# A gated recurrence and a PReLU network on one core: first-chunk scores in halves and quads, keys transposed by VectorE and DMA, weights in wider pieces

## The chip, the cores and the metric

The kernel runs on one core of a Trainium2 chip. A core has TensorE for matrix products, VectorE and ScalarE for elementwise work, GpSimd, and SyncE, which only issues transfers; 16 DMA engines move data for all of them. The time is the device time of one execution in microseconds, as a median of several runs.

## The reference

Two parts follow each other. The first is a recurrence with a gate for every key dimension, over 4 batches x 8 heads, 768 positions, 48 dimensions; the second is a network with a PReLU.

```python
f = 1.0 / (1.0 + np.exp(-f_logit))
for t in range(S):
    state = f[:, :, t, :, None] * state + einsum('bhd,bhde->...', k[:, :, t], v[:, :, t])   # outer product
    y[:, :, t] = einsum('bhd,bhde->bhe', q[:, :, t], state)
x = y.transpose(0, 2, 1, 3).reshape(3072, 384)
h = x @ w_in                                   # 384 -> 2048
g = np.maximum(h, 0.0) + alpha * np.minimum(h, 0.0)
out = g @ w_out                                # 2048 -> 384
```

## The kernel before

Positions are cut into six chunks of 128 (NC = 6) and batches into two pairs, which gives 12 steps (bp, c), all first chunks (c = 0) ahead. A step goes through four stages written as generators: `prepare` (gates and their products), `carry` (what passes between blocks, and the state), `attend` (scores inside blocks, output y) and `network`. A string of letters sets the order in which the pieces of the stages are issued: P and Q are prepare of this and the next step, O is carry, S is attend, n is the network of the step before, a and w load the input weights, b and v the output weights. TensorE, VectorE and ScalarE follow this order exactly.

Within a chunk, scores are formed in blocks of 32 positions. The gate products between two positions of a block are built by quads of four positions: `qd` for pairs in one quad, and `us` for pairs in different quads, where one product is kept for every distance m between quads, up to seven.

```python
# prepare
q4 = us[:, :, 0:DB]...                       # distance 1
def earlier(m):                              # distance m from distance m-1, m = 2..7
    nc.vector.tensor_tensor(us[... UO[m] ...], us[... skip ...], fq[:, :, 1:1 + n]..., ALU.mult)
k4 = work.tile([128, W], F32, ...)           # k times the gates to the end of its quad
nc.vector.tensor_tensor(k4, k, kr..., ALU.mult)
# q3: q times the gates since the start of the block, ks, kh: k times the gates to the end of the block
```

In `carry`, the gated keys `ks` are transposed on TensorE and copied by ScalarE, and multiplied with the values:

```python
pk = pair(f"pk_{i}")
for u in range(U):
    for hp in range(HP):
        nc.tensor.transpose(pk[:, u, hp * 128:(hp + 1) * 128], ks[...], ident)
ksn = work.tile([128, U, HP * 128], F32, tag="ksn", ..., bufs=1)
for u in range(U):
    nc.scalar.copy(ksn[:, u], pk[:, u])
...
nc.tensor.matmul(pd[64 * par:64 * par + 64, cc, o:o + D],
                 lhsT=ksn[s_, u, hp * 128 + 64 * par:hp * 128 + 64 * par + 64], rhs=vs[...])
```

In `attend`, raw is k times qd, qu is k4 times us, and copies under a mask put the wanted parts into `ad`; `ad` and the other parts go into A, and A times the values gives py, then y. Ten small DMAs place y as xT for the network:

```python
nc.tensor.matmul(raw[...], lhsT=k[...], rhs=qd[r_, g])                       # 80 columns
nc.tensor.matmul(qu[...], lhsT=k4[...], rhs=us[r_, g, 4:UW])                 # 112 columns
for m in range(1, NB):                                                       # seven copies
    nc.vector.copy_predicated(ad[:, u, :, :, 4 * m:DB], mquad[...], qu[...])
...
(nc.sync if hd % 2 else nc.scalar).dma_start(out=xT[...], in_=y[p0:p0 + n, :, hd // 2])
```

The network multiplies xT with w_in (ph, eight groups of 12 matmuls), forms g on ScalarE and VectorE, and multiplies with w_out (po, 64 matmuls).

Both weights arrive as 64-bit words from which the kernel takes the float32 value in two parts: ScalarE and VectorE work out the leading and the remaining part of a piece of WP = 512 columns, and a GpSimd DMA with addition joins them:

```python
def both(n):
    nc.gpsimd.dma_start(out=flat[:, n:n + WP], in_=got.pop(n)[1], accum_op=ALU.add)
```

Of the kernel before, what the change touches and what calls it, by code (L numbers as in the profile page):

```python
# [8 lines left out]
F32 = mybir.dt.float32  # L9
I16 = mybir.dt.int16  # L10
# [11 lines left out]
U = 2  # L22
# [3 lines left out]
WP = 512  # L26
RAWS, TOPS, POWERS, LEADS = 5, 3, 2, 4
# [3 lines left out]
def kernel(  # L31
# [27 lines left out]

    nc = tc.nc  # L60
# [11 lines left out]
    NJ = C // DB  # L72
    UO = [0, 0]
    for m in range(1, NB):
        UO.append(UO[-1] + (DB if m == 1 else DB - 4 * m))
    UW = UO.pop()
    QO = [0]
# [46 lines left out]
    for m in range(1, NB):  # L124
        lo = UO[m] + (4 if m == 1 else 0)
        n = NB - m
        nc.gpsimd.tensor_copy(mquad[:, lo:lo + 4 * n].rearrange("p (i r) -> p i r", r=4),
                              inq[:, 0:n].unsqueeze(2).broadcast_to((128, n, 4)))
    ad = const.tile([128, U, 2, HP, DB], F32, tag="ad", name="ad")
# [12 lines left out]

    def load_weights(dst, src, name):

        flat = dst.rearrange("p a n -> p (a n)")
        ks = NK if dst is w_in_sb else 1
        per = flat.shape[1] // ks
        todo = [k * per + j for j in range(0, per, WP) for k in range(ks)]
        got = {}

        def upper(n):
            raw = work.tile([128, WP, 4], I16, tag="raw", name=f"{name}_raw{n}", bufs=RAWS)
            nc.sync.dma_start(out=raw.rearrange("p n four -> p (n four)")[:, 0:4 * WP - 1],
                              in_=src[:, n:n + WP].bitcast(I16)[:, 1:4 * WP])

            top = raw[:, :, 2]
            pos = work.tile([128, WP], I16, tag="pos", name=f"{name}_pos{n}", bufs=TOPS)
            nc.scalar.activation(pos, top, AF.Relu, bias=bias[:, 0:1], scale=8.0)
            neg = work.tile([128, WP], I16, tag="wneg", name=f"{name}_neg{n}", bufs=TOPS)
            nc.scalar.activation(neg, top.bitcast(U16), AF.Relu, bias=bias[:, 1:2], scale=8.0)  # L170
            got[n] = raw, pos, neg

        def lead(n):
            raw, pos, neg = got[n]
            t = work.tile([128, WP], BF16, tag="lead", name=f"{name}_lead{n}", bufs=LEADS)
            nc.vector.tensor_tensor(t, pos.bitcast(BF16), neg.bitcast(BF16), ALU.subtract)
            got[n] = raw, t

        def power(n):
            raw, t = got[n]  # L180
            p = work.tile([128, WP], BF16, tag="power", name=f"{name}_power{n}", bufs=POWERS)
            nc.vector.tensor_scalar(p.bitcast(I16), t.bitcast(I16), -128, None, ALU.bitwise_and)
            got[n] = raw, t, p

        def rest(n):
            raw, t, p = got[n]
            low = raw.bitcast(U32)[:, :, 0]
            nc.vector.scalar_tensor_tensor(flat[:, n:n + WP], low, 2.0 ** -36, p, ALU.mult, ALU.mult)

        def both(n):  # L190
            nc.gpsimd.dma_start(out=flat[:, n:n + WP], in_=got.pop(n)[1], accum_op=ALU.add)  # L191

        def uppers():
            for n in todo:
                upper(n)
                yield

        def rests():
            for i, n in enumerate(todo + [None]):
                if n is not None:  # L200
                    lead(n)
                if i:
                    rest(todo[i - 1])
                if n is not None:
                    power(n)
                if i:
                    both(todo[i - 1])
                yield

        return uppers(), rests()  # L210
# [10 lines left out]

    def fill():

        while True:
            b = bank("warm")
            nc.tensor.matmul(b[:, 0:256], lhsT=ones[:, 0:128], rhs=ones[:, 0:256], start=True, stop=True)
            yield

    def prepare(bp, c, x):
# [42 lines left out]
        us = x["us"] = work.tile([128, G, UW], F32, tag="us", name=f"us_{i}", bufs=1)  # L272
        q4 = us[:, :, 0:DB].rearrange("p g (i r) -> p g i r", r=4)
        for r in range(4):
            nc.scalar.copy(q4[:, :, :, r], qdv[r][:, :, :, 0])  # L275
        nc.vector.tensor_tensor_scan(ps, fs, ones, 0.0, ALU.mult, ALU.add)
# [16 lines left out]

        k4 = x["k4"] = work.tile([128, W], F32, tag="k4", name=f"k4_{i}", bufs=1)
        nc.vector.tensor_tensor(k4, k, kr.rearrange("p n r -> p (n r)"), ALU.mult)
        earlier(2)
# [7 lines left out]

        def started(j):
            js = slice(j, G, 2)
            nc.vector.tensor_tensor(q3[:, :, 2 * j].rearrange("p g (i r) -> p g i r", r=4), q4[:, js],  # L307
                                    pre[:, js, 0:NB].unsqueeze(3).broadcast_to((128, GC, NB, 4)), ALU.mult)
# [9 lines left out]
        earlier(3)  # L318
        ended(1)
        earlier(4)  # L320
        started(1)
        earlier(5)
        yield
        earlier(6)
        nc.vector.tensor_tensor(ks[:, :, 0], kh, f32[:, 1:G:2].broadcast_to((128, GC, DB)), ALU.mult)
        earlier(7)
        nc.vector.tensor_tensor(q3[:, :, 1], q3[:, :, 2], f32[:, 0:G:2].broadcast_to((128, GC, DB)), ALU.mult)
# [10 lines left out]
        for cc in range(NC2):  # L338
            for par in range(2):
                nc.scalar.copy(A[halves(cc)[1], :, par * HP:(par + 1) * HP, CH * cc:CH * (cc + 1)],  # L340
                               q3[rows(par)].rearrange("p (u h c) s t -> p u h c (s t)", h=HP, c=NC2)[:, :, :, cc, 0:CH])
        yield

    def carry(bp, c, x):
# [4 lines left out]
        for u in range(U):  # L349
            for hp in range(HP):  # L350
                for cc in range(NC2):
                    g = (u * HP + hp) * NC2 + cc
                    o = (u * HP + hp) * DB
                    for par in range(2):
                        r_ = rows(par)
                        nc.tensor.matmul(off[CH * cc:CH * cc + DB, par, o:o + DB],  # L356
                                         lhsT=kh[r_, g], rhs=q3[r_, g, 2], start=True, stop=True)
        for cc in range(NC2):
# [6 lines left out]
        pk = pair(f"pk_{i}")  # L365
        for u in range(U):
            for hp in range(HP):
                a = (u * HP + hp) * NC2
                nc.tensor.transpose(pk[:, u, hp * 128:(hp + 1) * 128], ks[:, a:a + 2].rearrange("p c s t -> p (c s t)"), ident)  # L369
        ksn = work.tile([128, U, HP * 128], F32, tag="ksn", name=f"ksn_{i}", bufs=1)  # L370
        for u in range(U):
            nc.scalar.copy(ksn[:, u], pk[:, u])
        yield
        pd = pair(f"pd_{i}")
        for u in range(U):
            for hp in range(HP):
                for cc in range(NC2):
                    for par in range(2):
                        o = (u * HP + hp) * D
                        s_ = halves(cc)[0]  # L380
                        nc.tensor.matmul(pd[64 * par:64 * par + 64, cc, o:o + D],  # L381
                                         lhsT=ksn[s_, u, hp * 128 + 64 * par:hp * 128 + 64 * par + 64],
                                         rhs=vs[bp][s_, cc, u, (2 * hp + par) * D:(2 * hp + par + 1) * D], start=True, stop=True)

        def moved(cc):
# [6 lines left out]
            for par in range(2):  # L392
# [3 lines left out]
                else:  # L396
                    nc.vector.tensor_copy(then[:, :, par:H:2], now)  # L397
# [5 lines left out]
    def attend(bp, c, x):  # L403
# [4 lines left out]

        for u in range(U):
# [16 lines left out]
            for hp in range(HP):  # L426
                for j in range(NJ):
                    g = (u * HP + hp) * NJ + j
                    for par in range(2):
                        r_ = rows(par)  # L430
                        nc.tensor.matmul(qu[DB * j:DB * (j + 1), par, hp * UW + 4:(hp + 1) * UW],  # L431
                                         lhsT=k4[r_, g * DB:(g + 1) * DB], rhs=us[r_, g, 4:UW], start=True, stop=True)
            for m in range(1, NB):
                lo = UO[m] + (4 if m == 1 else 0)
                n = DB - 4 * m
                nc.vector.copy_predicated(  # L436
                    ad[:, u, :, :, 4 * m:DB],
                    mquad[:, lo:lo + n].bitcast(I32).unsqueeze(1).unsqueeze(1).broadcast_to((128, 2, HP, n)),
                    qu[:, :, 0:HP * UW].rearrange("p r (h x) -> p r h x", h=HP)[:, :, :, lo:lo + n])
# [26 lines left out]
        xT = x["T"] = work.tile([128, NK, T], F32, tag="xT", name=f"xT_{i}")  # L466
        for hd in range(H):
# [10 lines left out]
    def network(bp, c, x):  # L478
# [21 lines left out]
        for f in range(NF):  # L500
            for u in range(U):
                nc.tensor.matmul(po[u][:, 0:DM], lhsT=gs[f // 2][:, f % 2, u * C:(u + 1) * C], rhs=w_out_sb[:, f],  # L502
                                 start=(f == 0), stop=(f == NF - 1))
            if f % 4 == 3 and f != NF - 1:
                yield
        for u in range(U):
# [3 lines left out]
            nc.sync.dma_start(out=out[t0:t0 + C], in_=o)  # L510
        yield
# [7 lines left out]
        "P2 a2 P2 w a2 w P O w P a w S2 O w Q S2 a w a S a S Q w2",  # L519
        "a P w a w a P w n P a n w b v w S b v n b n O v b v n b v S P S n b O b v n b S v2 n2 S n b v Q b v b n v b v2 Q3 S n Q",  # L520
        "n2 O n S n2 S Q S n S O n2 Q n Q2 n P S n S Q n Q",
        "n S n2 S Q n2 O n S n S Q n O Q2 n Q S2 Q n3",
    )
    usual = "O n2 S n2 S2 n O n Q n Q n S n2 S Q n S Q2 n Q"
# [10 lines left out]
    with tc.manual_schedule(engines={mybir.EngineType.PE, mybir.EngineType.DVE, mybir.EngineType.Activation}):  # L535
        prep, car, att, net = begin(0)
        filling = fill()
        before = None
        for n in range(len(steps) + 1):
            coming, carried, following, after = begin(n + 1)  # L540
            on = pieces | {"P": prep, "O": car, "S": att, "z": filling, "n": before, "Q": coming}
# [60 lines left out]
```

## Time and profile before

| What | Value |
|---|---|
| Time, median of 3 runs | 659.77 us (658.13 to 659.81) |
| Span of the profiled execution | 658.4 us |
| PE (matmul) busy | 615.5 us, 93% |
| PEld (weight load) busy | 458.0 us, 70% |
| DVE (VectorE) busy | 420.2 us, 64% |
| ACT (ScalarE) busy | 267.0 us, 41% |
| POOL (GpSimd) busy | 69.9 us, 11% |
| Moved by DMA | 53.03 MB, 81 GB/s on average |

The profile calls TensorE PE and its weight loads PEld, VectorE DVE, ScalarE ACT, GpSimd POOL and SyncE SP; a q behind the name is the engine's queue of DMA issues. A line such as `L486 ph<-xT,w_in_sb` is the instruction of line 486 that writes ph from xT and w_in_sb. "Idle before" is the time in which the engine waited for it, and the arrow names what ended the wait. The granted clock is the share of TensorE's full clock that it was allowed in a stretch.

The shares are averages over a start, in which weights are prepared and little can be multiplied, and a long steady part. They have to be read by stage.

### The profile page before, as it was taken

To read this page: it belongs to the slowest core of one execution; us is meant where nothing else is said; L and a number is where in the kernel's file an instruction comes from. 1 tells how busy PE (TensorE), PEld (TensorE's weight loads), DVE (VectorE), ACT (ScalarE), POOL (GpSimd) and SP (SyncE) were. 2 spreads that over 40 slices of the span, in tenths; PEclk is the share of its full clock that TensorE was granted. 3 is DMA by queue.
4 is the path that set the end of the run, shared out by engine and by line. 5 is a ranking of instruction groups with operands and counts; after the bars stand their busy time and mean duration, and the time that the engine had idled before them with its cause. 6 is when DMAs were issued, how large, how long until landed. Compare 5 with 4: busy or idle time off the path is not lost.

```text
span 658.4 us, 17032 instructions
## 1 busy us (share of the span) xinstructions
PE 615.5 (93%) x7392; PEld 458.0 (70%) x7392; DVE 420.2 (64%) x897; ACT 267.0 (41%) x493; POOL 69.9 (11%) x109
## 2 busy tenths in 40 slices
PE   0548899999999999999999999999999999999997
PEld 0436766866876876876876876876876786786874
DVE  5999889693863685685585586486387486360220
ACT  5855882543443242451451550550460451431210
POOL 8222332000010000000000001001001000000000
PEclk9857999999999999999999999999999999999999
DMA  6979986122212122112013113023023011001000
GB/s 225 302 207 269 282 233 159 35 65 73 66 37 68 35 52 87 33 40 86 28 53 81 31 62 81 26 66 80 26 66 81 26 34 25 26 2 25 24 1 24
DMA packets 29129, 53.03 MB, mean 81 GB/s; under 512 B 4320, under 2 KB 16864, under 8 KB 29056
## 3 DMA queue, kind: packets, MB, share of 16 engines
q0 software_dynamic: 9616, 27.92, 15.4%
q1 hardware_dynamic: 13584, 21.63, 10.6%
q10 hardware_dynamic: 5856, 2.40, 1.7%
q8 instruction: 58, 0.95, 0.6%
q14 instruction: 15, 0.12, 0.1%
HBM read 36.21 MB, written 4.72 MB: 62 GB/s over the span
## 4 chain that ended last, share of the span: by engine, by line
PE 84%; issue 7%; POOL 4%; DVE 2%; ACT 1%; DMA 1%; POOLq 0%
PE po L502 36%; PE ph L486 35%; PE py L456 3%; PE qu L431 3%; PE raw L416 3%; PE pk L369 2%; PE pd L381 2%; POOL w_in_sb L191 1%; PE off L356 1%; POOL w_out_sb L191 1%; DMA w_out_sb<-w_out_lead 1%; DVE us L289 0%; POOL vs L138 0%; ACT A L340 0%; POOL vs L247 0%
## 5 line engine op out<-in xcount | busy, mean ns | idle before, releaser
L486 PE MATMUL ph<-xT,w_in_sb 128*128 128x256 f32 x1152 | 264.3, 387 | 10.3 <-DMA xT<-y 10.3
L502 PE MATMUL po<-w_out_sb,g 128*128 128x384 f32 x768 | 253.0, 488 | 0.3 <-DMA w_out_sb<-w_out_lead 0.3
L486 PEld LDWEIGHTS ph<-xT,w_in_sb 128*128 128x128 f32 x1152 | 218.1, 192 | 44.7 <-DMA w_in_sb<-w_in_lead 11.3
L502 PEld LDWEIGHTS po<-w_out_sb,g 128*128 128x128 f32 x768 | 144.9, 190 | 97.7 <-DMA w_out_sb<-w_out_lead 0.9
L494 DVE SCALAR_TENSOR_TENSOR g<-neg,om,ph 128x256 f32<-128x256 f32 x192 | 83.1, 476 | 152.0 <-ACT neg L491 151.9
L491 ACT ACTIVATE neg<-ph 128x512 f32<-128x512 f32 x96 | 57.7, 601 | 152.8 <-PE ph L486 124.8
L508 ACT COPY o<-po 128x384 f32<-128x384 f32 x24 | 11.5, 478 | 115.2 <-PE po L502 115.2
L436 DVE COPY_PREDICATED ad<-mquad,qu 128x224 f32<-128x224 int32 (+6 forms) x168 | 50.3, 300 | 8.5 <-DVE ad L422 0.5
L465 ACT COPY y<-py 128x512 f32<-128x512 f32 x24 | 12.9, 591 | 81.2 <-PE py L456 81.2
L289 DVE TENSOR_TENSOR us<-us,fs 128x768 f32<-128x768 f32 (+2 forms) x72 | 44.5, 618 | 0.3
L422 DVE COPY_PREDICATED ad<-mraw,raw 128x256 f32<-128x256 int32 (+1 forms) x96 | 42.3, 441 | 2.7
L445 ACT COPY A<-ad 32x256 f32<-32x256 f32 x96 | 38.4, 400 | 3.8 <-DVE ad L436 2.5
L391 DVE TENSOR_TENSOR vs<-vs,f 48x768 f32<-48x768 f32 x20 | 19.1, 953 | 30.4 <-PE py L456 30.0
L275 ACT COPY us<-qd 128x256 f32<-128x256 f32 x48 | 29.6, 666 | 12.2 <-DVE qd L258 7.4
L258 DVE TENSOR_TENSOR qd<-qd,f 128x768 f32<-128x768 f32 (+2 forms) x36 | 27.1, 752 | 8.2 <-ACT qd L253 8.2
L340 ACT COPY A<-q 48x512 f32<-48x512 f32 x48 | 29.6, 617 | 6.3 <-DMA xT<-y 5.5
L237 POOL DMA_DIRECT2D k<-in_kT x11 | 8.4, 761 | 222.6 <-PE raw L416 197.6
L456 PEld LDWEIGHTS py<-A,vs 128*64 128x64 f32 x768 | 25.1, 145 | 7.2 <-issue 6.2
L431 PE MATMUL qu<-us,k 48*32 48x112 f32 x1536 | 26.4, 265 | 2.6 <-DVE us L289 1.7
L456 PE MATMUL py<-A,vs 128*64 128x64 f32 x768 | 26.9, 231 | 0.9 <-DVE vs L397 0.8
L356 PE MATMUL off<-q,kh 48*32 48x32 f32 x768 | 9.4, 199 | 18.3 <-DVE q L307 18.3
L416 PEld LDWEIGHTS raw<-qd,k 48*32 48x32 f32 x1536 | 18.1, 108 | 10.6 <-issue 10.2
(64 smaller groups left out, 451.1 us busy)
## 6 DMA issues: line engine op xcount, KB each, us to landing
w_in_raw<-in_w_in SPq DMA_DIRECT2D x12, 511.8 KB, 5.9
w_out_raw<-in_w_out SPq DMA_DIRECT2D x12, 511.8 KB, 5.8
f<-in_fT POOLq DMA_DIRECT2D x11, 512.0 KB, 4.1
q<-in_qT POOLq DMA_DIRECT2D x11, 512.0 KB, 4.1
k<-in_kT POOLq DMA_DIRECT2D x11, 512.0 KB, 4.3
out<-o SPq DMA_DIRECT2D x24, 192.0 KB, 1.9
vs<-in_v POOLq DMA_DIRECT2D x22, 192.0 KB, 3.5
w_in_sb<-w_in_lead POOLq DMA_DIRECT2D x12, 256.0 KB, 6.1
```

Of the source, the lines that this page charges most:

```text
L275: nc.scalar.copy(q4[:, :, :, r], qdv[r][:, :, :, 0])
L289: nc.vector.tensor_tensor(us[:, :, UO[m]:UO[m] + 4 * n].rearrange("p g (i r) -> p g i r", r=4), us[:, :, skip:skip + 4 * n].rearrange("p g ...
L416: nc.tensor.matmul(raw[DB * j:DB * (j + 1), par, hp * C:hp * C + QW], lhsT=k[r_, g * DB:(g + 1) * DB], rhs=qd[r_, g], start=True, stop=True)
L422: nc.vector.copy_predicated(adu[:, :, :, d:4], mraw[:, d, :, d:4].bitcast(I32).unsqueeze(1).broadcast_to((128, H, NB, n)), rv[:, :, QO[d]: ...
L431: nc.tensor.matmul(qu[DB * j:DB * (j + 1), par, hp * UW + 4:(hp + 1) * UW], lhsT=k4[r_, g * DB:(g + 1) * DB], rhs=us[r_, g, 4:UW], start=T ...
L436: nc.vector.copy_predicated(ad[:, u, :, :, 4 * m:DB], mquad[:, lo:lo + n].bitcast(I32).unsqueeze(1).unsqueeze(1).broadcast_to((128, 2, HP, ...
L445: nc.scalar.copy(A[s_, u, :, s_], ad[s_, u].rearrange("p r h t -> p (r h) t"))
L456: nc.tensor.matmul(py[64 * par:64 * par + 64, u, o:o + CH], lhsT=vs[bp][:, cc, u, hd * D:hd * D + 64], rhs=A[:, u, par * HP + hp, CH * cc: ...
L486: nc.tensor.matmul(ph[:, j * T:(j + 1) * T], lhsT=w_in_sb[:, kt, (f + j) * 128:(f + j + 1) * 128], rhs=xT[:, kt], start=(kt == 0), stop=(k ...
L491: nc.scalar.activation(neg, phv, AF.Relu, scale=-1.0)
L494: nc.vector.scalar_tensor_tensor(g[:, j], neg[:, j], om[:, f + j:f + j + 1], phv[:, j], ALU.mult, ALU.add)
L502: nc.tensor.matmul(po[u][:, 0:DM], lhsT=gs[f // 2][:, f % 2, u * C:(u + 1) * C], rhs=w_out_sb[:, f], start=(f == 0), stop=(f == NF - 1))
```

## The change

It has several parts.

- **First chunk (c = 0, two of the 12 steps).** Nothing comes from earlier chunks, so fewer products are needed and there is room to form the scores differently: inside halves of 16 positions by quads (three distances rather than seven), and between the two halves of a block by 64 more small matmuls of 16 columns (k16, q16), which are written next to off and copied by ScalarE. qu becomes 52 columns wide, and three copies under a mask take the place of seven. Half of q3 that the first chunk does not use is not formed. The first copy of pd into the state moves from VectorE to ScalarE.
- **Gated keys (c > 0, ten steps).** The transpose of ks leaves TensorE: VectorE transposes blocks of 32x32, and 16 DMAs of SyncE put the blocks in place in ksn. pk and its copies are kept for c = 0. pd loads 48 weight columns rather than 64.
- **First xT.** In the first step, matmuls with a shifted identity (dense) form xT in place of the ten DMAs.
- **Weights.** Pieces of 768 rather than 512, those of w_in across the three row groups at once, so that one piece serves one pair of network columns; the first piece is added on VectorE.
- **Order.** The strings of letters are new. The last step finishes its first 128 rows before the others.

```diff
-WP = 512
-RAWS, TOPS, POWERS, LEADS = 5, 3, 2, 4
+WP = 768
+AT_ONCE = 1
+RAWS, TOPS, POWERS, LEADS = 4, 3, 1, 4
...
+            t = by_row(got.pop(n))
+            if n < at_once:
+                nc.vector.tensor_tensor(of(n), of(n), t, ALU.add)
+            else:
+                nc.gpsimd.dma_start(out=of(n), in_=t, accum_op=ALU.add)
...
         ended(0)
-        earlier(3)
+        if c:
+            earlier(3)
+        else:
+            near(2, 1)
         ended(1)
-        earlier(4)
+        if c:
+            earlier(4)
+        else:
+            nc.vector.tensor_tensor(k16[...], k4[...], g16[...], ALU.mult)
...
+        if c:
+            kt = work.tile([128, 2 * WP], F32, tag="raw", name=f"kt_{i}", bufs=RAWS)
+            nc.vector.transpose(kt[:, 0:W], ks.rearrange("p g s t -> p (g s t)"))
+            ksn = x["ksn"] = work.tile([128, U, HP * 128], F32, tag="ksn", name=f"ksn_{i}", bufs=1)
+            for a in range(4):
+                n = min(32, D - 32 * (a % 2))
+                for b in range(NJ):
+                    nc.sync.dma_start(out=ksn[32 * b:32 * (b + 1)]...[:, :, 32 * a:32 * a + n],
+                                      in_=kt[32 * a:32 * (a + 1), 0:W]...[:, :, b, 0:n])
...
+        if not c:
+            ... nc.tensor.matmul(off[DB * j:DB * (j + 1), par, o:o + 16], lhsT=x["k16"][r_, g], rhs=x["q16"][r_, g])
+            nc.scalar.copy(ad[:, u, :, :, 16:DB], off[...])
...
-                        nc.tensor.matmul(pd[64 * par:64 * par + 64, cc, o:o + D],
-                                         lhsT=ksn[s_, u, hp * 128 + 64 * par:hp * 128 + 64 * par + 64],
+                        nc.tensor.matmul(pd[rows(par), cc, o:o + D],
+                                         lhsT=ksn[s_, u, hp * 128 + 64 * par:hp * 128 + 64 * par + D],
...
-                    nc.vector.tensor_copy(then[:, :, par:H:2], now)
+                    nc.scalar.copy(then[:, :, par:H:2], now)
...
+        if not (bp or c):
+            for kt in range(NK):
+                b = bank(f"xt{kt}_{i}")
+                for hp in pairs:
+                    nc.tensor.matmul(b[:, 0:T], lhsT=dense[:, o:o + 128], rhs=y[:, :, hp], ...)
+                nc.scalar.copy(xT[:, kt], b[:, 0:T])
+            return
...
     first = (
-        "P2 a2 P2 w a2 w P O w P a w S2 O w Q S2 a w a S a S Q w2",
-        "a P w a w a P w n P a n w b v w S b v n b n O v b v n b v S P S n b O b v n b S v2 n2 S n b v Q b v b n v b v2 Q3 S n Q",
-        "n2 O n S n2 S Q S n S O n2 Q n Q2 n P S n S Q n Q",
-        "n S n2 S Q n2 O n S n S Q n O Q2 n Q S2 Q n3",
+        "P2 a P w P a P a w O P w S a w S Q a O a w S2 Q w S Q S",
+        "P a w a P w2 b n2 v O n b2 v S n v n P S b S v b n S v n b v Q b n b n v O v n v Q3 S2 n2 Q2",
+        "O n2 S n2 S Q S2 n3 O n Q n Q2 n S2 n Q2 n",
+        "n O n2 S n2 S Q n O Q n2 S Q n S n S Q2 S Q n2",
     )
-    usual = "O n2 S n2 S2 n O n Q n Q n S n2 S Q n S Q2 n Q"
+    usual = "O n S n2 S n2 O n Q n Q2 n2 S3 n Q S n Q n Q"
```

## The prediction

> **What bounds the kernel now.** I read the page first (which engine is full, and when), then the busy time by stage, then TensorE's timeline of the start, then the chain that ended last for one steady step, and the waits at the end.
>
> The windows (columns: window, length, then busy us and instruction count of PE, PEld, DVE, ACT, POOL, then granted clock, DMA share, GB/s):
>
> ```profile
> 30.00:45.00 15.00, 8.09 (x192) 7.12 (x192) 14.00 (x32) 9.29 (x18) 4.62 (x6) 0.50 0.71 197
> 45.00:60.00 15.00, 9.13 (x88) 6.78 (x88) 14.34 (x29) 8.96 (x15) 5.03 (x6) 0.65 0.98 273
> 90.00:105.00 15.00, 14.71 (x103) 9.00 (x102) 13.29 (x24) 9.38 (x15) 7.16 (x9) 1.00 1.03 252
> 287.00:337.00 50.00, 50.00 (x616) 37.19 (x615) 33.22 (x70) 19.09 (x37) 3.38 (x5) 1.00 0.20 57
> ```
>
> There are two regimes. From about 60 us on TensorE is full at full clock and VectorE has a third of its time free. Before that VectorE is full (14.0 and 14.3 of 15 us), TensorE is half idle at half clock, and the DMA engines are nearly full as well. So a step in the steady part is worth exactly its TensorE time, and the start is worth what VectorE, the transfers and the cold clock let through.
>
> The timeline of TensorE at the start (start, length, instruction, idle before it):
>
> ```profile
> 36.23 3.47 PE L456 MATMUL py<-A,vs 128*64 128x64 f32 x60 [0.78 <-DVE vs L397]
> 48.50 2.04 PE L486 MATMUL ph<-xT,w_in_sb 128*128 128x256 f32 x4 [8.80 <-DMA xT<-y]
> 52.04 6.24 PE L486 MATMUL ph<-xT,w_in_sb 128*128 128x256 f32 x20 [1.50 <-DMA xT<-y]
> 61.85 7.13 PE L486 MATMUL ph<-xT,w_in_sb 128*128 128x256 f32 x24
> 109.97 5.34 PE L486 MATMUL ph<-xT,w_in_sb 128*128 128x256 f32 x24
> ```
>
> The first network step waits 8.8 us for the transposed activations (xT) that come by DMA, then runs 24 matmuls in 8.28 us and the next 24 in 7.13 us where the steady part takes 5.18 to 5.38: the clock is cold. At 109.97 the second network step begins; I use it as the finish of the start.
>
> The chain, one steady step (start, length, work):
>
> ```profile
> 311.49 0.69 PE off L356 x50
> 312.17 1.02 PE pk L369 x8
> 313.20 5.18 PE ph L486 x24
> 318.38 0.85 PE raw L416 x60
> 319.22 0.84 PE qu L431 x61
> 320.07 5.38 PE ph L486 x24
> ...
> 361.82 0.69 PE off L356 x50
> ```
>
> A step is 361.82 - 311.49 = 50.33 us, all TensorE. Two readings matter later: ph x24 takes 5.18 after pk but 5.38 after qu, so going from packed small matmuls back to full ones costs 0.20; and raw (80 columns) costs as much as qu (112 columns), so a narrower qu saves nothing there.
>
> [...]granted clock 0.50 from 30 to 52 us, 1.00 later, and a dip to 0.57 at 62 to 66. [...]xT<-y, 512-byte rows, lands 2.6 to 3.3 us after issue. The new pieces are 128 and 64 bytes.
>
> **The change part by part.**
>
> *Gated keys (10 of 12 steps).* The eight transposes pk go: 1.02 us. The ph behind them now follows off and pays 0.20 for the switch. Net 0.82 x 10 = 8.2 us, all on the path. In place come one VectorE transpose of 128x1024 (the other 128x1024 operations take 1.2 us; VectorE has 17 us free per step) and 16 DMAs from SyncE. ScalarE loses two copies (1.07 us), off the path.
>
> *pd with 48 weight columns instead of 64.* 1.08 us per 64 matmuls; I allow 0.05 each for 12 steps: 0.5 us.
>
> *First chunk, two steps.* TensorE gets 64 more small matmuls of 16 columns; 64 off matmuls cost 0.69, so +0.7 per step. qu falls from 112 to 52 columns: 0 by the reading above. VectorE: the six products of us (0.94+0.81+0.68+0.55+0.41+0.28 = 3.7) become three of 256 elements (0.41), two of 512 (0.68) and two tiny ones, 2.9; two q3 products are halved, -0.55; seven predicated copies (2.3) become three (estimated 0.95), -1.35; two copies of pd move to ScalarE, -1.1. Sum -3.8 per step, -7.6 for both.
>
> *Weights.* 24 pieces of 512 at 0.42+0.69+0.29 = 1.40 give 33.6 us of VectorE. With 256 elements more[...] and the others in proportion, a piece of 768 is 0.59+0.95+0.40 = 1.94; 16 of them are 31.0. One add on VectorE (0.95) replaces the first accumulating DMA. Net -1.6. The bytes stay.
>
> *First xT by TensorE.* Six matmuls of 256 columns; cold ones took 2.04/4 = 0.51, so 3.1 us, and a copy of 0.4 behind; this replaces the DMAs (y ready at 41.5, first ph at 48.5, third part at 52.0). But the order of the changed kernel puts eight A copies (3.3 us) and four us copies (2.1 us) on ScalarE ahead of y, behind weight work that itself waits for the larger pieces. Followed by hand with the durations above, VectorE ends the first chunk's score copies at about 35 us as before (it has processed half as much weight again by then), y is ready at about 46, first ph at about 48.8. So the wait for xT is not removed from the end of the chain; its place is taken by ScalarE's queue. What is gained comes after it: no second wait for xT (1.5)[...], and 9 us less VectorE work.
>
> *Sum of the start.* Before: from 48.5, full-speed work up to the next network step is 41.4 (network) + 9.2 (attention with its switches) = 50.6, ending at 99.1; it ended at 109.97, so 10.9 us were lost, which the timeline confirms: cold clock 3.1 + 1.8, waits 1.5 + 1.7 + 2.2 + 0.5. After: 48.8 + 51.3 (0.7 more work) + losses: cold clock 3, a wait of some 2.5 for VectorE's second q3 (about 57 us, because ph can do only two groups first in the new order), 1 for smaller ones: 106.6. Gain 3.4 us.
>
> *End.* The last step finishes the first half of its rows early and stores it, but the last half's copy (0.48) and store (about 2.4) remain: 0.
>
> Total: 8.2 + 0.5 + 3.4 = 12.1 us; the extra 0.7 of step two is inside the 3.4 and that of step one is before 48.8. 659.8 - 12.1 = **647.6 us**.
>
> **Rivals.**
>
> *The DMAs arrive late for pd.* VectorE can finish the transpose about 4 us before the step ends (its last products ended at 360.3 of 361.8 here after it had waited 4.8 us for py, and the new order has py one po group, 5.2 us, earlier; the transpose adds 1.2); pd starts some 17.5 us into the next step: a window of 21.5. SyncE issued five xT DMAs in 4.41 us, 0.88 each, so 16 need 14.1, two stores 1.0 and landing 3: 18.1. It fits by 3 us. If an issue costs 1.3 us, as at the start (6.62 for five), 24.8 are needed: 3.3 us lost in each of ten steps, about 680. Against it: those slow issues were under a full DMA load, and the steady share is 0.2.
>
> *The transfers bound the start.* DMA share is near 1 from 45 to 60 and from 90 to 105 us, and the last w_out piece came just in time (0.3 us waited). The bytes are the same. Then the start gains nothing: 651.
>
> *VectorE was the true bound of the start.* Then its 9 us come through nearly whole: 642.
>
> **Range and chances.** The 8.7 us of the steady part are read from one chain and vary by 1. The start is -1 to +9. So 641 to 654 holds most. 2% is 13.2 us, a limit of 646.6, one microsecond from my value: faster 0.43, same 0.53, slower 0.04 (the late DMAs).
>
> **What would show it.** Steady step 49.4 to 49.5 with no wait at pd, and ph x24 after off at 5.38: right. An idle stretch before pd, released by ksn DMAs: the first rival. Second network step at about 106.6 us: right; at 110: the transfers, with waits for w_in_sb or w_out_sb; at 102: VectorE. First ph well before 48 us would make my reading of ScalarE's queue wrong. off16 should be 0.7 us and narrow qu 0.84.

## The result and the profile after

| | Before | After |
|---|---|---|
| Median time | 659.79 us | 651.6 us (650.77 to 653.02, 4 runs) |
| Ratio, 95% interval | | 0.9879 [0.9847, 0.991] |
| Span of the profiled execution | 658.4 us | 649.0 us |
| First ph | 48.50 us | 52.98 us |
| Second network step begins (in the new order its off stands ahead of the first ph) | 109.97 us | 109.67 us |
| One steady step | 50.33 us | 49.47 us |

The windows of the changed kernel, in the same stretches and columns as those shown of before:

```profile
30.00:45.00 15.00, 5.91 (x207) 5.07 (x204) 12.32 (x25) 8.49 (x15) 4.66 (x6) 1.00 0.73 188
45.00:60.00 15.00, 13.02 (x266) 11.20 (x262) 13.18 (x26) 10.92 (x19) 4.59 (x5) 0.89 0.90 238
90.00:105.00 15.00, 15.00 (x166) 9.48 (x165) 14.87 (x24) 6.49 (x12) 4.54 (x6) 1.00 0.77 204
287.00:337.00 50.00, 50.00 (x611) 36.81 (x610) 34.99 (x73) 18.95 (x37) 3.38 (x5) 1.00 0.27 65
```

VectorE is no longer full from 30 to 45 us (12.3 of 15 instead of 14.0), yet TensorE does less there than before (5.9 us instead of 8.1). So it is not VectorE's work that holds TensorE up for longer than before. The timeline of TensorE in the start says where (start, length, instruction, idle before it):

```profile
18.47 1.08 PE L442 MATMUL off<-q,kh 48*32 48x32 f32 x64 [18.47 <-DVE q L366]
20.10 1.43 PE L452 MATMUL off<-us 48*32 48x16 f32 x128 [0.55 <-DVE us L400]
21.46 1.97 PE L469 MATMUL pk<-ident,ks 128*128 128x128 f32 x8
23.36 0.75 PE L518 MATMUL raw<-qd,k 48*32 48x80 f32 x22
26.22 0.96 PE L518 MATMUL raw<-qd,k 48*32 48x80 f32 x38 [2.10 <-issue]
...
29.41 0.74 PE L518 MATMUL raw<-qd,k 48*32 48x80 f32 x21 [1.34 <-DVE ad L524]
33.29 0.91 PE L518 MATMUL raw<-qd,k 48*32 48x80 f32 x38 [3.14 <-issue]
...
37.89 1.20 PE L482 MATMUL pd<-vs,ksn 64*48 64x48 f32 x44 [0.80 <-issue]
42.66 0.48 PE L572 MATMUL py<-A,vs 128*64 128x64 f32 x4 [3.57 <-ACT A L561]
...
48.64 4.51 PE L590 MATMUL xt<-y,dense 128*128 128x256 f32 x12 [1.98 <-ACT y L581]
52.98 5.35 PE L614 MATMUL ph<-xT,w_in_sb 128*128 128x256 f32 x24
...
76.11 9.72 PE L614 MATMUL ph<-xT,w_in_sb 128*128 128x256 f32 x36 [3.17 <-issue]
...
109.67 0.76 PE L442 MATMUL off<-q,kh 48*32 48x32 f32 x64
```

Four stalls (2.10, 3.14, 0.80 and 3.17 us) stand in the middle of runs of like matmuls or ahead of such a run, and the profile names no releaser for them, only "issue". The kernel before has two lines with this word up to here; the third line below is VectorE's:

```profile
28.77 1.04 PE L416 MATMUL raw<-qd,k 48*32 48x80 f32 x43 [0.67 <-issue]
80.20 1.15 PE L381 MATMUL pd<-vs,ksn 64*64 64x48 f32 x64 [2.18 <-issue]
78.25 1.85 DVE L422 COPY_PREDICATED ad<-mraw,raw 128x256 f32<-128x256 int32 x4
```

Only the first is of the same kind. The 2.18 us ahead of pd end just after VectorE's copies of raw (78.25 + 1.85 = 80.10), so by the times pd waited there for its buffer pair.

The steady part is as foreseen. One step of the changed kernel, and the last network; then the last network of the kernel before:

```profile
356.58 0.76 PE L442 MATMUL off<-q,kh 48*32 48x32 f32 x64
357.26 2.86 PE L614 MATMUL ph<-xT,w_in_sb 128*128 128x256 f32 x12
360.05 0.92 PE L518 MATMUL raw<-qd,k 48*32 48x80 f32 x64
360.91 1.08 PE L533 MATMUL qu<-us,k 48*32 48x112 f32 x64
...
374.36 0.94 PE L482 MATMUL pd<-vs,ksn 64*48 64x48 f32 x64
...
406.05 0.76 PE L442 MATMUL off<-q,kh 48*32 48x32 f32 x64
...
603.83 20.88 PE L614 MATMUL ph<-xT,w_in_sb 128*128 128x256 f32 x96
```

```profile
613.52 20.88 PE L486 MATMUL ph<-xT,w_in_sb 128*128 128x256 f32 x96
```

The step is 406.05 - 356.58 = 49.47 us, pk is gone, and pd follows without a wait: the 16 DMAs of the keys come in time. The last network begins 603.83 - 109.67 = 494.16 us after the second one; before, it was 613.52 - 109.97 = 503.55. So by the two profiled executions ten steps gave 9.4 us, the start 0.3, and the end (45.17 us after the start of the last network instead of 44.88) took 0.3 back.

**What the stalls could be.** If one counts matmuls from the beginning of TensorE's work, the first stall of the changed kernel comes after 64 (off) + 128 (off16) + 8 (pk) + 22 (raw) = 222 of them, the second after 222 + 38 + 4 + 64 + 21 = 349, the third after 476 and the fourth after 1112. In the kernel before, 0.67 us stands after 64 + 8 + 64 + 64 + 21 = 221. The spacing is 127 matmuls (222 and seven such spacings are 1111), with their weight loads 254 instructions. And close ahead of each, the DMA queue called "instruction" moves one packet. The transfers of the changed kernel from 23 to 24 us (queue: packets, MB, share of the 16 engines):

```profile
## 3 DMA queue, kind: packets, MB, share of 16 engines
q0 software_dynamic: 46, 0.14, 58.5%
q1 hardware_dynamic: 14, 0.03, 16.5%
q8 instruction: 1, 0.02, 7.6%
```

This packet starts at about 23.35; those ahead of the other three stalls start at 30.8, 35.6 and 73.8. TensorE goes on at 26.22, 33.29, 37.89 and 76.11, 2.3 to 2.9 us later. In all the runs of this document, every "issue" stall that does not stand at the first pd of a step lies within 3 matmuls of 222 plus a multiple of 127, with such a packet 2.2 to 3.1 us ahead of its end. (The 2.18 us of the kernel before have their last packet at 74.5, 5.7 us ahead.) Over the whole run this queue (q8) moved 60 packets and 0.98 MB, 16 KB each, while TensorE ran 7580 matmuls and as many weight loads: one packet for 253 of these instructions. (Before: 58 packets for 7392 matmuls, one for 255.) That is about the spacing of the stalls (254).

Hence theory 1: TensorE runs out of instructions where small matmuls follow one another without a wait, because the next block arrives late among the weights' transfers. Its rivals: ScalarE's queue alone sets the first ph (theory 2, the prediction's reading), or VectorE or the transfers set the end of the start whatever happens ahead.

### The profile page after: what moved, and what is told of

Its sections match the earlier page's. It is cut to its first block, busy times and chain, and to the rows that moved or that the text cites. A ratio compares the mean times of both kernels' runs of the same rounds, so it can differ in the third digit from the quotient of the medians.

```text
span 649.0 us, 17589 instructions
## 1 busy us (share of the span) xinstructions
PE 608.0 (94%) x7580; PEld 451.1 (69%) x7580; DVE 423.6 (65%) x866; ACT 254.9 (39%) x466; POOL 67.7 (10%) x114
## 4 chain that ended last, share of the span: by engine, by line
PE 93%; DVE 2%; issue 2%; ACT 2%; DMA 1%; DVEq 0%; ACTq 0%
PE ph L614 40%; PE po L638 39%; PE raw L518 3%; PE py L572 3%; PE qu L533 3%; PE pd L482 2%; PE off L442 1%; PE xt L590 1%; DMA f<-in_fT 1%; ACT A L561 0%; PE pk L469 0%; PE off L452 0%; ACT us L312 0%; DVE ad L524 0%; DVE us L319 0%
## 5 line engine op out<-in xcount | busy, mean ns | idle before, releaser
L539 DVE COPY_PREDICATED ad<-mquad,qu 128x224 f32<-128x224 int32 (+6 forms) x140 | 41.9, 299 | 6.2
L328 DVE TENSOR_TENSOR us<-us,fs 128x768 f32<-128x768 f32 (+5 forms) x60 | 37.0, 617 | 0.3
L415 ACT COPY A<-q 48x512 f32<-48x512 f32 x44 | 27.1, 616 | 9.4 <-DVE f L410 4.6
L518 PE MATMUL raw<-qd,k 48*32 48x80 f32 x1536 | 24.1, 243 | 7.2 <-issue 5.2
L533 PE MATMUL qu<-us,k 48*32 48x112 f32 (+1 forms) x1536 | 25.5, 259 | 0.0
```

Source lines behind the costliest of these rows:

```text
L328: nc.vector.tensor_tensor(us[:, :, UO[m]:UO[m] + 4 * n].rearrange("p g (i r) -> p g i r", r=4), us[:, :, skip:skip + 4 * n].rearrange("p g ...
L518: nc.tensor.matmul(raw[DB * j:DB * (j + 1), par, hp * C:hp * C + QW], lhsT=k[r_, g * DB:(g + 1) * DB], rhs=qd[r_, g], start=True, stop=True)
L533: nc.tensor.matmul(qu[DB * j:DB * (j + 1), par, hp * QS + 4:hp * QS + QL], lhsT=k4[r_, g * DB:(g + 1) * DB], rhs=us[r_, g, 4:QL], start=Tr ...
L539: nc.vector.copy_predicated(ad[:, u, :, :, 4 * m:DB], mquad[:, lo:lo + n].bitcast(I32).unsqueeze(1).unsqueeze(1).broadcast_to((128, 2, HP, ...
```

## The experiments

Where a run leaves out work, it is said; times are medians, ratios are to the kernel before of the same chip.

**The gated keys alone** (and pd with 48 columns), in the order of the kernel before:

```diff
 kernel before
+        if c: kt = transpose of ks by VectorE; 16 DMAs to ksn    # after the fifth piece of prepare
-        pk = pair(...)                                          # every step
+        if not c: pk = pair(...)
-   pd[64 * par:64 * par + 64, ...]  lhsT=ksn[..., 64 columns]
+   pd[rows(par), ...]               lhsT=ksn[..., 48 columns]
```

> The kernel before with the new path of the gated keys alone (VectorE blocks and 16 DMAs for c > 0, pd with 48 weight columns), old order, old weights, old first chunk. If the whole gain of the change is its steady part, as the trace of the changed kernel reads (step 50.33 to 49.47, start unchanged), the time falls by about 9 us, to 651, as far as the whole change. If the start of the change does bring the 3.4 us of my prediction, this kernel stays some 3 us above the changed one, at 655. If the old order leaves the DMAs too little time, pd waits and the step stays above 50.

Measured 649.32 us, 0.9849 [0.9831, 0.9866]: at least about the gain of the whole change (the intervals overlap). From the second network step to the last one it takes 493.15 us, a little less than the changed kernel's 494.16, so the new order of the steady steps costs a little: most of them take 49.3 us here and 49.47 in the changed kernel.

**The rest alone**: the changed kernel with pk in every step.

```diff
-        if c: kt = ..., 16 DMAs
-        if not c: pk = pair(...)
+        if True:  pk = pair(...)
```

> The changed kernel with the old path of the gated keys in every step (transposes on TensorE, two ScalarE copies); new first chunk, weights, first xT, order and pd with 48 columns stay. If the start brings nothing: about 657.5 (only the narrower pd, 0.2 us in each of 12 steps, is left). If the start brings the predicted 3.4 us: about 654.

Measured 662.0 us, 1.0038 [1.0024, 1.0052]. pd is 0.21 us shorter in a steady step here too; with that inside, the start, the weights and the order together are a small loss. In the profiled execution the start is not where it lies: the second network step begins at 108.97, but a steady step takes 50.56 us instead of 50.33, so the new order costs some 0.4 us a step when pk stays in it.

**The changed kernel without off16.** The scores between the two halves of each block of the first chunk are left out, with the ScalarE copies of them.

```diff
-        if not c: 64 matmuls off[..., 16 columns] <- k16, q16; 2 copies ad <- off
```

> The changed kernel without the 64 matmuls of 16 columns between halves and their copies, in both first-chunk steps; the scores between halves of a block are left out of the first chunk's output, all VectorE work stays. If TensorE's waits in raw and pd are its instruction supply[...], removing 128 of them shifts or removes one wait: the sum of the waits without a visible cause between 20 and 40 us falls by 2 to 3 us and the first ph comes 2 to 4 us earlier. If those waits have another cause, they stay and only 1.4 us of matmul time goes.

Measured 645.86 us, 0.9794 [0.9774, 0.9813], from two runs. TensorE's timeline of this kernel:

```profile
22.05 1.34 PE L505 MATMUL raw<-qd,k 48*32 48x80 f32 x64 [0.63 <-ACT A L447]
...
27.23 1.33 PE L505 MATMUL raw<-qd,k 48*32 48x80 f32 x64 [3.00 <-DVE ad L511]
...
48.28 5.34 PE L601 MATMUL ph<-xT,w_in_sb 128*128 128x256 f32 x24
...
104.61 0.76 PE L442 MATMUL off<-q,kh 48*32 48x32 f32 x64
```

Neither raw is broken any more. The first waits for nothing but a copy (0.63 us); the second waits 3.00 us for VectorE, and by theory 1 the next block has time to arrive meanwhile. The first ph comes at 48.28, 4.7 us earlier, though the matmuls left out took only 1.4. (py still waits 3.57 us for ScalarE: theory 2 has a part in what remains.) Two stalls are left on the same spacing: 0.84 us inside pd, after 348 matmuls, and 4.27 us at the ph after 856. Here are the weight load (PEld) and the matmuls of that ph:

```profile
66.92 0.19 PEld L601 LDWEIGHTS ph<-xT,w_in_sb 128*128 128x128 f32 x1
71.26 9.50 PE L601 MATMUL ph<-xT,w_in_sb 128*128 128x256 f32 x36 [4.27 <-issue]
```

The load of the first weights from w_in_sb ran 4.3 us ahead of the matmul, so this stall is no wait for a piece of w_in.

**ScalarE's copies of A earlier**, in the changed kernel:

```diff
-        "... O P w S a w S Q a O a w S2 Q w S Q S"
+        "... O P w S a w S Q a S2 O w S Q S a w Q"
```

> The changed kernel with one string of the order altered: in the first step ScalarE copies the scores into A before the copy of pd and before the next piece of weights. If ScalarE's queue sets the first ph (at 53.0 now), it comes about 4 us earlier, near 49, and the time falls by 1 to 4 us, as far as VectorE lets the next attention through. If the waits of TensorE in raw and pd (5 us from 24 to 38 us) set it, the first ph moves by less than 1.5 us. If a later bound (VectorE, transfers, instruction supply) sets the end of the start, the first ph moves and the second network step does not.

Measured 656.4 us, 0.9947 [0.9926, 0.9967]: 5 us slower than the changed kernel, although the first ph comes at 49.66, 3.3 us earlier. One line of VectorE and one of TensorE tell why:

```profile
52.03 0.56 DVE L205 TENSOR_TENSOR w_in_lead<-w_in_pos,w_in_neg 128x768 bf16<-128x768 bf16 x1 [5.92 <-ACT w_in_neg L199]
```

```profile
59.70 1.08 PE L442 MATMUL off<-q,kh 48*32 48x32 f32 x64 [4.69 <-DVE q L366]
```

The weight pieces that ScalarE now does after y held VectorE for 5.92 us, and what VectorE did later held the second chunk for 4.69 us: theory 2 is right on the first ph and wrong on the end of the start.

**off16 issued twice**, the same results written again:

```diff
         if not c: 64 matmuls off <- k16, q16
+                  the same 64 again
```

> The 128 off16 matmuls of a first-chunk step are issued twice (same results), nothing else changes. Theory 1 (TensorE runs out of instructions): in the changed kernel the stalls stand after matmul 222 and after matmul 349 of the stream; 128 more small matmuls move the places: the stall at 222 now falls inside the second round of off16, the one at 349 into the first raw, and one more comes before pd. First ph at 55.5 to 57 instead of 53.0, total 655 to 657. Theory 2 (only ScalarE's queue sets the first ph): TensorE's extra 1.2 to 1.4 us per step are partly hidden, first ph at most 54.2, total 652 to 654.

Measured 661.04 us, 1.0009 [0.9994, 1.0023]. In TensorE's timeline (L461 is the repetition):

```profile
21.36 0.48 PE L461 MATMUL off<-us 48*32 48x16 f32 x27
25.05 1.24 PE L461 MATMUL off<-us 48*32 48x16 f32 x97 [3.22 <-issue]
...
51.02 5.34 PE L623 MATMUL ph<-xT,w_in_sb 128*128 128x256 f32 x24
...
59.58 0.56 PE L461 MATMUL off<-us 48*32 48x16 f32 x44
64.77 1.01 PE L461 MATMUL off<-us 48*32 48x16 f32 x82 [4.63 <-issue]
```

The place is as theory 1 said: after 64 + 128 + 31 = 223 matmuls, now in the middle of the repetition. The sizes were not: the later stalls of the first chunk fell to 0.25 and 0.67 us, so the first ph came earlier (51.02), not later, and the whole loss of 9.4 us against the changed kernel (8 us between the profiled executions) arose in the second step, from 51.02 to the last ph group at 83.93 (32.9 us, against 23.1). It is 1.45 us of waiting for VectorE ahead of off16, 1.2 of matmuls, a stall of 4.63, and slower matmuls behind it: pk 1.97 instead of 1.09, ph x12 4.54 instead of 2.75 (the granted clock reads 0.50 while pk runs). Some 10 us. So 4.63 us went in the stall itself, and 2.7 more in the pk and ph behind it.

**The first chunk's scores as before** (seven products, seven masked copies, no off16), all else as changed:

```diff
-        if not c: halves of 16, k16, q16, off16, qu of 52 columns, three masked copies
+        as for c > 0: us with seven distances, qu of 112 columns, seven masked copies
```

> The changed kernel with the first chunk's scores as before (seven products and seven masked copies, qu 112 columns, no off16); all else of the change stays. Theory 1 (instruction supply): VectorE gets about 5 us of work per first-chunk step back, yet the stalls after matmul 222 vanish or hide behind waits for VectorE, so first ph comes at 48 to 50.5 instead of 53.0 and the total is 646 to 649. Rival (VectorE's relief by the quads of 16 is worth its time): first ph at 55 or later, total 654 to 657.

Measured 649.65 us, 0.9842 [0.982, 0.9864]; first ph at 49.56. It has a span of 647.7 us where the changed kernel has 649.0, with more work for VectorE in each of the first steps. No stall stands inside a raw; one of 2.91 us ahead of ph x36, after 856 matmuls, remains. So what the quads of 16 save on VectorE is no more than what they cost TensorE; that it is less is not shown, since the two intervals overlap. The expected total was up to 0.7 us too low: raw, qu and pk of the second step waited for VectorE again, 0.4 to 1.2 us each.

**The first xT by DMAs again**, in the changed kernel:

```diff
-        if not (bp or c): 6 matmuls with dense, 3 copies
+        ten DMAs, as in the other steps
```

> The changed kernel with the first step's xT brought by DMAs again. If the transposition by TensorE is worth what I assumed (the DMA way took 7.0 us from y to the first ph and a second wait of 1.5; the new one 5.2 us): first ph at 55 and a cold or interrupted start behind it, total 654 to 656. If the transfers or VectorE set the second network step anyway, total 651 to 652.5.

Measured 655.75 us, 0.9923 [0.9898, 0.9947]. TensorE:

```profile
58.03 2.05 PE L614 MATMUL ph<-xT,w_in_sb 128*128 128x256 f32 x4 [12.11 <-DMA xT<-y]
...
81.94 2.43 PE L614 MATMUL ph<-xT,w_in_sb 128*128 128x256 f32 x10
86.01 5.77 PE L614 MATMUL ph<-xT,w_in_sb 128*128 128x256 f32 x26 [1.65 <-issue]
```

The matmuls are worth some 4 us to this order of work. The second stall tells more: twelve matmuls (xt) fewer have run by then, and the stall that stood ahead of ph x36 now stands after ten of them. A wait for a piece of w_in would stand at the beginning of a group of twelve; this one goes by the count of instructions.

**Without the weights' traffic**: only the first piece of w_in is loaded, and all weights are computed from it by the same instructions. The loads of the 15 other pieces are left out.

```diff
-        raw = work.tile(...); dma_start(raw <- piece n)     # every piece
+        raw = one;            dma_start only for the first piece of w_in
-RAWS = 4                                            # buffers for raw pieces
+RAWS = 3
```

> Leaves out the loading of 15 of the 16 weight pieces: all weights are computed from the first piece of w_in, with the same work on ScalarE, VectorE and the accumulating DMAs. If the stalls of TensorE after matmul 222 and 349 (2.1 and 3.1 us) are fetches of instructions that queue behind the weight load: they fall to about 1 us each or vanish, and first ph comes at 46 to 49. If a fetch takes its time whatever the load: stalls of 2 to 3 us stay. If they have to do with the weights' transfers only through ScalarE's order: stalls stay and the wait of py for ScalarE goes.

Measured 642.56 us, 0.973 [0.9705, 0.9756]. TensorE:

```profile
23.43 1.52 PE L521 MATMUL raw<-qd,k 48*32 48x80 f32 x64
...
27.33 0.47 PE L521 MATMUL raw<-qd,k 48*32 48x80 f32 x21 [1.80 <-DVE ad L527]
28.45 0.90 PE L521 MATMUL raw<-qd,k 48*32 48x80 f32 x38 [0.65 <-issue]
...
45.69 5.34 PE L617 MATMUL ph<-xT,w_in_sb 128*128 128x256 f32 x24
...
69.49 8.04 PE L617 MATMUL ph<-xT,w_in_sb 128*128 128x256 f32 x36 [1.53 <-issue]
```

The same instructions in the same order, and the four stalls are 0, 0.65, 0 and 1.53 us instead of 2.10, 3.14, 0.80 and 3.17. The fetch that started at 23.35 starts at about 21.9 here, with TensorE's work up to it the same within 0.1 us. (In three other runs with the same instructions up to this place and all loads, those with pk in every step, with the copies of A earlier and with xT by DMAs, it started at 22.6 to 22.75 and the first stall took 1.0 to 1.55 us: the load delays it by varying amounts.) From the packet to TensorE's going on it takes 2.2 us here, about as long as with the load, so what the load changes is when the packet moves. From 18 to 24 us the DMA engines are busy to 0.46 here; in the changed kernel they are nearly full (0.98). How the load delays the packet was not shown. The 7.3 us of the first ph aren't all due to the fetches: ScalarE and VectorE no longer wait for pieces either.

**Attempts to combine.** The gated keys alone, with xT by TensorE and the first pd copies on ScalarE:

```diff
 keys alone
+        if not (bp or c): 6 matmuls with dense, 3 copies
-                    nc.vector.tensor_copy(then[...], now)
+                    nc.scalar.copy(then[...], now)
```

> The kernel before with the gated keys' new path (the earlier run of that alone took 649.3 us), with the first xT by TensorE and the first two copies of pd on ScalarE; pieces of 512, the first chunk's scores and the order of work stay as before. If the start is bound by the wait for xT: first ph at about 46 instead of 47.9 with no second wait (2.5 us), total 645 to 647. If VectorE, full from 15 to 60 us, bounds it: the next raw waits for us as before, total 648 to 649.5.

Measured 655.15 us, 0.9934 [0.992, 0.9948], a clear miss. ScalarE's timeline and then TensorE's:

```profile
34.18 0.96 ACT L415 COPY vs<-pd 48x384 f32<-48x384 f32 x2 [5.46 <-PE pd L399]
```

```profile
66.58 1.75 PE L449 MATMUL qu<-us,k 48*32 48x112 f32 x64 [8.63 <-DVE us L294]
```

In the old order the copies of pd stand ahead of the next chunk's gates and of weight pieces, so ScalarE idled 5.46 us in front of them; the chain through VectorE then cost TensorE 8.63 us. Copies that took 0.55 us each on VectorE in the kernel before cost ScalarE 5.46 us of idle time here, in front of the first of them. The two edits weren't tried apart.

The changed kernel with the old scores, and the copies of A ahead of one weight piece:

```diff
-        "... Q a O a w S2 Q w S Q S"
+        "... Q a O S2 a w Q w S Q S"
```

> The changed kernel without the quads of 16 (that alone took 649.7 us), and in the first step ScalarE makes the copies of A ahead of one weight piece instead of behind it. ScalarE-queue theory: py starts 2 us earlier, first ph at 47.5, and the displaced weight piece costs little; total 647.5 to 649. If the weights' pieces set the end of the start (the last ph groups wait 2.9 us for w_in): total 649.5 to 651 in spite of an earlier first ph.

Measured 649.53 us, 0.9851 [0.9836, 0.9866]. py starts 1.6 us earlier, but y still stands behind a weight piece and the four us copies on ScalarE, and the first ph comes at 50.77. The total fell at the lower edge of the second range, but not for its reason (the first ph came later, not earlier); there is no measurable difference from the run without this edit.

The same with the old order of the steady steps, and then with y ahead of the us copies:

```diff
-    usual = "O n S n2 S n2 O n Q n Q2 n2 S3 n Q S n Q n Q"
+    usual = "O n2 S n2 S2 n O n Q n Q n S n2 S Q n S Q2 n Q"
```

> The kernel of the run before (changed kernel without the quads of 16, copies of A early; 649.5 us), with the order of the steady steps as in the kernel before (24 ph ahead of the first raw). Read from the steady steps of two runs, the old order takes 49.32 us and the new one 49.42 to 49.43 per step: 7 to 8 such steps, 0.8 us: total 648.7, just under the 649.3 of the gated keys alone. If the blocks of keys now land late for pd (their transposition starts at the end of the step in both): 2 us or more slower.

> As the run before in this call, and in the first step ScalarE copies y (from py) ahead of the four us copies of the next chunk (2.1 us), instead of behind them. If the path from y through xT to the first ph bounds the start: first ph 2 us earlier and total about 647. If VectorE's work on the next chunk, which starts from the us copies, bounds it: the earlier ph is followed by a longer wait for VectorE at the next off and pk, total the same as the other or up to 2 us more.

Measured 648.23 us, 0.983 [0.9814, 0.9847], and 648.89 us, 0.9838 [0.9821, 0.9854]. A steady step of the first, in TensorE's timeline:

```profile
304.82 0.76 PE L412 MATMUL off<-q,kh 48*32 48x32 f32 x64
305.50 5.45 PE L571 MATMUL ph<-xT,w_in_sb 128*128 128x256 f32 x24
...
354.12 0.76 PE L412 MATMUL off<-q,kh 48*32 48x32 f32 x64
```

That is 49.30 us instead of 49.47, and the best time of the runs that leave nothing out, 3.4 us under the median of the changed kernel. The second edit, shown by its end of the first string,

```diff
-        "... Q a O S2 a w Q w S Q S"
+        "... Q a O S2 a w Q w S2 Q"
```

missed its aim: the us copies belong to the Q ahead of it, so they still ran at 42.23, y at 44.36, and xt started at 45.58 as in the other. It tests nothing; whether y ahead of us pays wasn't tried alone.

## Why the prediction came out as it did

The total lay in the range (651.6 in 641 to 654) for the reason given first, the steady part. The term of the start was mis-sized: of the 3.4 us foreseen 0.3 came, and these 3.1 us are most of the 4 us between 647.6 and 651.6.

- **Gated keys, 8.2 us, and pd, 0.5: right in mechanism.** A step fell by 0.86 us as the sum had it (0.82 + 0.05), but by other terms: pk -0.93, pd -0.21 rather than -0.05, the switch behind qu and pk +0.10, and +0.18 for raw and qu, as the first raw of a step takes 0.86 instead of 0.69 (the cause isn't shown). Over ten steps the two traces differ by 9.4 us, 0.7 more than foreseen. The rival of late DMAs did not come true: an issue took 0.61 us (I had allowed 0.88), the landing 1.9 us.
- **First ph at about 48.8: wrong by 4.2 us** (52.98). This is the step that failed. The prediction took "64 more small matmuls" for +0.7 us, first by a slip: the program's 64 fp32 matmuls are 128 in the trace, as the 32 of off are 64 there, so they cost 1.4 us in the first step and 1.2 in the second. Above all it took them for time only. By theory 1 they pushed TensorE past the end of its supply of instructions inside the first raw, and again inside the second: 2.10 and 3.14 us, where the profile before had 0.67 us of this kind. The same slip of counting stands in the xT term: six matmuls are twelve in the trace, and from their start to the first ph it took 4.34 us instead of 3.1 + 0.4. Without off16, the first ph came at 48.28 and the second network step at 104.61, 0.5 and 2 us below the values on record (48.8 and 106.6).
- **ScalarE's queue takes the place of the wait for xT: right in part.** py waited 3.57 us and xt 1.98 us for ScalarE, and moving its copies moved the first ph. But its work can't be moved for nothing, as the run with the copies of A earlier shows (656.4 us).
- **From the first ph to the second network step 57.8 us: nearly right (56.7), but by luck.** The second wait for xT was gone and ph x24 ran in 5.35 us, about as in a steady step (5.45). The 3 us allowed for the cold clock and 2.5 for VectorE's second q3 were not lost there; 3.17 were lost by another stall for instructions ahead of ph x36.
- **Narrow qu, 0: wrong in the good direction.** 52 columns took 0.75 us (64.69 to 65.44) instead of 1.00.
- **VectorE's relief, 3.8 us a step: it came, and is worth little.** By the durations of its instructions it was some 4.6 us a step: the masked copies are made twice a step, for both batches of a pair, and fell by 2.4 us rather than 1.35. The weights took 2.7 us less instead of 1.6. But VectorE's idle time rose while TensorE stood still. With the old scores the total was no worse.
- **End, 0: nearly right** (0.3 us slower). The prediction's own sum, 659.8 - 12.1, is 647.7.
- **Rivals.** "The transfers bound the start" named the second network step at 110 and 651 us, and both came. But the sign I gave for it, waits for w_in_sb or w_out_sb, isn't what stands there; the transfers acted through the fetches of instructions (the first two stalls: 2.10 and 3.14 us with all loads, 0 and 0.65 with most left out). That VectorE was the true bound has the run with the old scores against it.

What stays open: why the first stall comes after just 222 matmuls, how early a fetch is asked for, and what fills the 2.2 to 3.1 us between the packet and TensorE's next matmul. The wait ahead of pd in the first chunk (1.22 us in the changed kernel) has the same name, "issue", but ends with VectorE's copies of the last raw (34.40 + 1.88 = 36.28, pd at 36.38); so by the times it is a wait for the buffer pair, like the 2.18 us of the kernel before, and not a fetch; no run tested it.

## What to carry to other kernels

Work added to TensorE can have a price in instructions as well as in time: here 128 small matmuls, 1.4 us together, brought stalls of 2.10 and 3.14 us in the first step. Where dozens of small matmuls run without a wait while the DMA engines are full, count them, and look for "issue" stalls at a fixed spacing (here 127 matmuls) and for packets of the instruction queue just ahead (here 2.2 to 3.1 us before the end of the stall). Relief for an engine that looks full need not reach the total: some 4.6 us less of VectorE's work in each of two steps stood in the kernel of 651.6 us, and with the old scores it took 649.65. An instruction moved to another queue can take its wait along, as the copies of pd did here (5.46 us). Try the parts of a change apart: here one part brought all the gain that could be measured.

## What the runs showed of the hardware

- The stalls of TensorE at a spacing of 127 matmuls, each with a 16 KB packet of the instruction queue ahead of its end, took up to 4.6 us among the weights' transfers (off16 issued twice), in the changed kernel 0.8 to 3.2; with most of the weights' loads left out, 0 to 0.65 at the same places in the first chunk and 1.53 in the second step. In the steady part, at a DMA share of 0.27, no such stall appears.
- From the start of such a packet to TensorE's next matmul it took 2.2 to 3.1 us, with and without the load.
- VectorE's transposition of 128x1024 fp32 in blocks of 32x32 took 1.25 us, about as long as a product of that size (1.2).
- The granted clock does not tell here how fast TensorE works: while pd x44 ran (from 37.9 and 37.2 us) it reads 1.00 in the changed kernel and 0.50 in the run with pk in every step, and the 44 matmuls took 1.20 us in both. In the steady part 64 of them take 0.94.
